# Forward and backward of a spectral mixer with a channel MLP: eight early w2^T blocks with ScalarE copies, input-gradient passes ordered tile by tile, and three small moves

## The chip, the cores and the metric

One core of one Trainium2 chip. The metric is the device time of one execution in microseconds. The kernel before took 1412.49 us (median of 3 runs, 1410.25 to 1417.26). The engines are called as in the profile: PE is TensorE (matmul) and PEld its weight loads, DVE is VectorE, ACT is ScalarE, POOL is GpSimd, SP is SyncE; SP and POOL issue most of the DMAs.

## The reference

The kernel computes one forward pass and all gradients of it (2048 tokens, width 1024, hidden width 3584, bfloat16).

```python
mod = (silu(c) @ w_mod).reshape(1, 6, 1, -1)          # sa, ca, ga, sb, cb, gb
h = layernorm(x) * (1 + ca) + sa
x = x + ga * irfft2(rfft2(h) * (w_r + 1j * w_i))      # spectral part
h = layernorm(x) * (1 + cb) + sb
x = x + gb * (gelu(layernorm(h) @ w1 + b1) @ w2 + b2) # channel MLP
out, vjp = jax.vjp(f, A_x, A_w_r, A_w_i, B_w1, B_b1, B_w2, B_b2, c, w_mod)
return out, *vjp(grad_out)
```

## The kernel before, in words

Everything is written with Tile, a framework in which the program states operations on tiles and a planner lays out, before the run and by its own estimates of durations, the order of the instructions of each engine, the engine of each `nc.any` operation (ScalarE or VectorE), and the waits. Each engine then works strictly through its list. The program steers the planner by its own order (earlier lines have priority), by `tc.high_priority()`, by `tc.issue_after(ins)` and by `behind(ins, later)` (both put an instruction after another on one engine). Tiles with the same `tag` share one place in memory: a new tile waits for the last reader of the one before it. PSUM has the tags `s` and `d` with two banks each and `f` with four.

The stages, in the order of time:

1. *Start (0 to 122 us).* Six products `silu(c) @ w_mod` (`mod_block`), grad_out transposed and scaled into `gBoT`, and the first blocks of `ph_part` (L809). One block `fc` of `ph_part` is grad_out x w2^T for 128 hidden columns: four token groups j, each of 8 matmuls 128x512 at L814 into an `f` bank (`pp`), a copy to SBUF (L820, tiles `pho` and `phr`, `phr` being the place of every fourth block), and one POOL store to `d_ph`. The weights come through a ring of four `wt` places, by a transposing DMA of SP (`load_w2t`). `PH_EARLY = 6` (L824) blocks stand in a loop that also loads the weights four blocks ahead, a seventh stands alone behind it (L834), and its last matmul is `early_pe`. Meanwhile VectorE and ScalarE normalise x in four chunks (`ln_dve`, `ln_mix`, `norm_act`) and VectorE folds them by symmetry into `fbuf` (`fold_tok`, `fold_d`, `fold_pair`, all through L194). Chunk 2 is complete only after the last `fold_pair`.
2. *Spectral part, forward (to 222 us).* `spectral_core`: the `pu` matmuls (L531, L538) read `fbuf`; the first group is put behind `early_pe`. Blocks of `ph_part` that are written further down (L897 on) are used by the planner as filling wherever a spectral matmul is not ready.
3. *Rest of `ph_part` (to 344 us)*, then the MLP forward (to 733 us): `z_block` (pz, L951, PSUM `s` and `d` in turn; gelu and its derivative on ScalarE and VectorE) and `bo_pass` (pbo, L1005), in a hand-written order. At the end of each `bo_pass`, `pa` (an `s`/`d`/`f` bank; `d` here) holds column sums that go into `gacc` (its memory is called w2sD in the profile): L1027 copies it for b = 0.
4. *Input-gradient passes (733 to 941 us).* `pg_pass(b, h)`, L1099: for token block b (4) and half h (2), four PSUM tiles `pgs[i]` are summed over 7 groups g of hidden columns, 4 matmuls each (L1105). A step is one (g, i), four matmuls; a pass has 28 steps, g outer and i inner. The operand `gzs[b, g]` is loaded by SP into a ring of eight places (L1081). At the end ScalarE copies the four tiles with a row sum (L1121, `gn3a`, `gn3b`). For b < 2 and h = 1 ScalarE also sums each `gzs[b, g]` for the bias gradient (L1115). For b > 0 column sums (`acc3a`, L217) are put between steps at fixed places. Successive passes take their PSUM tiles from six banks in turn, so the third tile of a pass needs the bank of an early tile of the pass before. VectorE and ScalarE meanwhile work on `ln_bwd` (L1199 to L1204).
5. *Weight gradient of w2 and spectral part, backward (to 1200 us and beyond)*, with 16-matmul pieces (`fill(n)`) of the w2 and w1 weight gradients (L1239, L1464) put between. `consume_bwd(i, ...)`, i = 0 to 3: unfolds, multiplies with the normalised x (`tmp`, called ct), LayerNorm backward, store; then `fill((4, 7, 6, 8)[i])`, the column sum `halves_sum(accCA, tmp)` (L217, 8 matmuls), `fill(2)`.
6. *End (to 1411 us).* `accSA` sums (L214), `sr` (L1519, tag `px0`, which the fourth chunk's x, called xt, holds before it) takes them scaled by ScalarE (L1521); then the remaining w1 pieces, whose results are copied at L1468 and stored.

Of the kernel before, what the change touches and what calls it, by code (L numbers as in the profile page):

```python
# [10 lines left out]
FP32 = mybir.dt.float32  # L11
# [6 lines left out]
P = 128  # L18
S = 2048
D = 1024  # L20
# [3 lines left out]
NFC = F // P  # L24
KH = D // 2
# [5 lines left out]
NB = 4  # L31
# [4 lines left out]
def kernel(  # L36
# [24 lines left out]
    nc = tc.nc  # L61
# [4 lines left out]
    reg = ctx.enter_context(tc.tile_pool(name="reg", bufs=1))  # L66
# [12 lines left out]
    def ps_f(name):  # L79
        return psum.tile([P, 512], FP32, tag="f", name=name, bufs=4)  # L80
# [44 lines left out]
    def chunk_rows(dt, i):  # L125
        return dt[4 * i * P:4 * (i + 1) * P, :].rearrange("(q p) d -> p q d", p=P)
# [213 lines left out]
    def load_w2t(fc):  # L340
        w2t_in[0] = nc.sync.dma_start_transpose(out=wt[:, fc % 4], in_=B_w2[fc * P:(fc + 1) * P, :])
        w2ts.append(w2t_in[0])
# [461 lines left out]
    last_pe = [None]  # L804

    def ordered():
        return tc.issue_after(last_pe[0].ins)

    def ph_part(fc, js):  # L809
        ph2 = phs[fc % 4]  # L810
        for j in js:
            pp = ps_f("pp")
            for cch in range(NDC):
                last_pe[0] = nc.tensor.matmul(pp[:], lhsT=wt[:, fc % 4, cch, :], rhs=gBoT[j][:, cch, :],  # L814
                                              start=(cch == 0), stop=(cch == NDC - 1))
            q = (0, 2, 3, 1)[j]
            ov = ph2[:, :, q * P:(q + 1) * P]
            pv = pp[:, :].rearrange("p (i w) -> p i w", w=P)
            with tc.high_priority():
                nc.any.tensor_copy(out=ov, in_=pv)  # L820
        if js[-1] == 3:
            nc.gpsimd.dma_start(out=d_ph[fc * P:(fc + 1) * P, :], in_=ph2.rearrange("p i w -> p (i w)"))

    PH_EARLY = 6  # L824
    late_mods = [(r, h) for r in (2, 3, 4) for h in range(2)]
    for fc in range(PH_EARLY):
        ph_part(fc, (0, 1, 2, 3))
# [3 lines left out]
                for r, h in late_mods[3 * (fc // 2 - 1):3 * (fc // 2)]:  # L831
                    mod_block(r, h)

    ph_part(PH_EARLY, (0, 1, 2, 3))  # L834
    early_pe = last_pe[0]

    for i in range(4):
# [56 lines left out]
            w1s.append(wtile)  # L894

    PH_KEEP = NFC - 4
    for fc in range(PH_EARLY + 1, NFC):  # L897
        if fc >= PH_EARLY + 4:
            load_w2t(fc)
            load_w1({24: 1, 25: 1, 27: 5}.get(fc, 0))  # L900
        ph_part(fc, (0, 1, 2, 3) if fc < PH_KEEP else (0, 1))
# [10 lines left out]
    gacc = px1t[:, 1].rearrange("p a b -> p (a b)").bitcast(FP32)  # L912
# [76 lines left out]
    def bo_pass(b, h):  # L989
        cs_ = slice(h * KH, (h + 1) * KH)  # L990
        pbs = [((ps_s, ps_d)[k % 2] if (b, h) == (NB - 1, 0) else ps_f)("pbo") for k in range(4)]
        for i in range(4):
            with ordered():
                last_pe[0] = nc.tensor.matmul(pbs[i][:], lhsT=ones_bf[32 * i:32 * i + 1, :],
                                              rhs=b2_row[32 * i:32 * i + 1, cs_], start=True, stop=False,
                                              tile_position=(32 * i, 0))
        for g in range(7):
            n = (2 * b + h) * 7 + g
            w2_load(n + 3 if b == NB - 1 else n)
            wp = w2p[n % 4]  # L1000
            hh = hh_slots[(b * 7 + g) % 11]
            for i in range(4):
                for k in range(4):
                    with ordered():
                        last_pe[0] = nc.tensor.matmul(pbs[i][:], lhsT=hh[:, k, i * P:(i + 1) * P], rhs=wp[:, k, :],  # L1005
                                                      start=False, stop=(g == 6 and k == 3))
            if g < 6:
                yield
        bo, x1t, go = (otile[0][:, k] for k in range(3))
        nc.sync.dma_start(out=x1t, in_=chunk_rows(d_x1, b)[:, :, cs_])  # L1010
        load_tok_half(go, grad_out, b, h)
        for i in range(4):
            with tc.high_priority():
                last_ev[0] = nc.scalar.copy(out=bo[:, i, :], in_=pbs[i][:])
        tt(go, go, bo, ALU.mult)
        tt(bo, bo, bcn(gb_row[:, cs_], 4), ALU.mult)
        tt(bo, bo, x1t, ALU.add)
        store_tok_half(out_0, bo, b, h)

        yield  # L1020
        pa = (ps_f if (b, h) in ((NB - 2, 1), (NB - 1, 1)) else ps_d)("pa")
        for i in range(4):
            with ordered():
                last_pe[0] = nc.tensor.matmul(pa[32 * i:32 * (i + 1), :], lhsT=ones_bf[:, 0:32], rhs=go[:, i, :], start=True, stop=True)
        with tc.high_priority():
            if b == 0:
                nc.vector.tensor_copy(out=gacc[:, cs_], in_=pa[:])  # L1027
            else:
                tt(gacc[:, cs_], gacc[:, cs_], pa[:], ALU.add)

# [65 lines left out]
    last_pg = [None]  # L1096
    sums_in = [[], [], []]

    def pg_pass(b, h, pool, before=lambda: ExitStack()):  # L1099
        pgs = [pool(k)("pg") for k in range(4)]  # L1100
        for g in range(7):
            for i in range(4):
                for k in range(4):
                    with before():
                        last_pg[0] = nc.tensor.matmul(pgs[i][:], lhsT=gzs[b, g][:, k, i * P:(i + 1) * P],  # L1105
                                                      rhs=w1Ts[g][:, k, h * KH:(h + 1) * KH],
                                                      start=(g == 0 and k == 0), stop=(g == 6 and k == 3))
                    last_pe[0] = last_pg[0]
                g0 = 3 if b == NB - 1 else 2
                if b > 0 and h == 0 and (g, i) in ((g0, 0), (g0 + 1, 2), (g0 + 2, 2)):  # L1110
                    for ins in sums_in[g - g0]:
                        behind(ins, last_pg[0])
                    sums_in[g - g0].clear()
            for k in range(4 if b < 2 and h == 1 else 0):
                nc.scalar.activation(out=gzs[b, g][:, k, :], in_=gzs[b, g][:, k, :], func=ACT.Identity,  # L1115
                                     accum_out=gb1_acc[:, g * 4 + k, b:b + 1])
            if g < 6:
                yield
        for i in range(4):
            with tc.high_priority():  # L1120
                nc.scalar.activation(out=gn3_of(b)[:, i, h * KH:(h + 1) * KH], in_=pgs[i][:], func=ACT.Identity,  # L1121
                                     accum_out=g_sums[b][:, h, i:i + 1])
        yield
# [248 lines left out]
    def consume_bwd(i, o4, tmp, tmp2, n1, eb):  # L1372
        if i == 0:
            accCA.append(ps_s("accCA"))
            nc.vector.tensor_copy(out=sacc, in_=eb[:, 0, :])
        elif i == 2:
            tt(sacc, sacc, eb[:, 0, :], ALU.add)
        unfold_d(o4, tmp)
        unfold_tok(o4, tmp)
        load_tok(n1, A_x, i, nc.gpsimd)  # L1380
        with tc.issue_after(last_po[0].ins):
            norm_act(n1, n1, 0, i)
        tt(tmp, o4, n1, ALU.mult)
# [92 lines left out]
    def fill(n):  # L1476
        for _ in range(n):
            next(todo)
        done[0] += n
# [36 lines left out]

    accSA = [ps_d("accSA0"), ps_d("accSA1")]
    colsum(accSA, sacc, True, True)
    sr = reg.tile([P, 2, 1, D], FP32, name="sr", tag="px0")  # L1519
    for h in range(2):  # L1520
        nc.scalar.mul(out=sr[0:1, 0, 0, h * KH:(h + 1) * KH], in_=accSA[h][0:1, :], mul=8.0)  # L1521
    unfold_d(sr[0:1, 0], sr[0:1, 1])
# [48 lines left out]
```

## Time and profile before

| what | value |
|---|---|
| median of 3 runs | 1412.49 us (1410.25 to 1417.26) |
| profiled execution | 1412.42 us, span 1410.6 us |
| mean granted TensorE clock | 0.992 |
| DMA | 333.22 MB, mean 236 GB/s |
| TensorE busy in slices of 35 us | 5, then 9 or more of ten throughout, 8 in one that holds the start of the spectral part |

The span runs from the first to the last instruction; the rest of the execution's time lies around it. In an order of time a row has start, length in us, engine, line, operation, out<-in, shape and count; in brackets stands the idle time before the first of them, and what ended it. A row of a list of waits has who waited, for whom, total us, times, longest. A row of windows has the stretch, its length, and the busy time of each engine in it, then the granted clock, the share of the DMA engines and GB/s.

### The profile page before, as it was taken

What the parts mean: (1) busy time and instruction counts of PE and PEld (TensorE: products, weight loads), DVE (VectorE), ACT (ScalarE), POOL (GpSimd) and SP (SyncE); (2) the same over time, 40 slices, a digit from 0 to 9 for tenths busy, and PEclk for the clock granted to TensorE, in tenths of its full rate; (3) what the DMA queues carried; (4) which work ended last, traced back from release to release, by engine and by line L of the source; (5) the groups of instructions that cost most, each with busy time, mean ns of one, the idle gap of its engine ahead of it and who ended that gap; (6) DMA issues with size and microseconds to landing.
All of it is one profiled execution on the core that took longest, in us unless ns stands there. A gap on an engine that the chain in (4) does not pass through costs nothing. (4 is left out here: it accounts for less than half of the span.)

```text
span 1410.6 us, 18696 instructions
## 1 busy us (share of the span) xinstructions
PE 1374.2 (97%) x6963; PEld 664.5 (47%) x6963; DVE 1072.4 (76%) x1507; ACT 739.2 (52%) x1059; POOL 351.2 (25%) x436
## 2 busy tenths in 40 slices
PE   5998999999999999999999999999999999999999
PEld 2545565444444444444444444444544565444444
DVE  5897889987978777887620688999498757979960
ACT  4774667667877765665314583243622444434311
POOL 5510623201112122112210010112345330322341
PEclk8899999999999999999999999999999999999999
DMA  9972666899787777696999499996689996897971
GB/s 330 301 234 57 176 165 200 265 283 350 256 258 242 229 242 249 189 287 224 298 271 232 138 237 321 259 259 209 197 265 288 261 253 173 218 250 189 286 270 38
DMA packets 361265, 333.22 MB, mean 236 GB/s; under 512 B 208026, under 2 KB 303152, under 8 KB 361046
## 3 DMA queue, kind: packets, MB, share of 16 engines
q1 hardware_dynamic: 319990, 206.01, 55.9%
q0 software_dynamic: 35424, 120.78, 24.5%
q10 hardware_dynamic: 5760, 5.25, 1.2%
q8 instruction: 54, 0.88, 0.3%
q14 instruction: 37, 0.30, 0.1%
HBM read 166.77 MB, written 115.92 MB: 200 GB/s over the span
## 5 line engine op out<-in xcount | busy, mean ns | idle before, releaser
L1105 PE MATMUL pg<-w1T,gzr 128*128 128x512 bf16 x896 | 196.0, 379 | 2.8 <-ACT gn3b L1121 2.8
L814 PE MATMUL pp<-gBoT,wt 128*128 128x512 bf16 x896 | 197.9, 380 | 0.8 <-DVE phr L820 0.4
L1464 PE MATMUL gw1acc<-gzh,n3n 128*128 128x512 bf16 x640 | 140.0, 379 | 0.2 <-DVE gwo L1468 0.2
L1105 PEld LDWEIGHTS <-gzr 128*128 128x128 bf16 x896 | 86.6, 98 | 111.1 <-issue 8.5
L1464 PEld LDWEIGHTS <-n3n 128*128 128x128 bf16 x896 | 87.3, 98 | 107.1 <-issue 3.3
L951 PEld LDWEIGHTS <-w 128*128 128x128 bf16 x896 | 87.2, 98 | 107.0 <-issue 2.5
L814 PEld LDWEIGHTS <-wt 128*128 128x128 bf16 x896 | 87.5, 98 | 104.0 <-issue 1.5
L951 PE MATMUL pz<-n3Tb,w 128*128 128x512 bf16 x448 | 99.2, 379 | 1.0 <-DVE w2sD L1027 1.0
L951 PE MATMUL pz<-n3Ta,w 128*128 128x512 bf16 x448 | 98.7, 379 | 0.0
L1005 PEld LDWEIGHTS <-hhA 128*128 128x128 bf16 x608 | 59.0, 98 | 73.1 <-issue 2.8
L1239 PE MATMUL gw2acc<-gB,hhsA 128*128 128x512 bf16 x416 | 92.2, 379 | 0.0
L954 ACT ACTIVATE gt<-pz,b_col 128x512 bf16<-128x512 f32 x112 | 72.8, 683 | 33.2 <-PE pz L951 33.0
L962 ACT ACTIVATE gt<-gt 128x2048 bf16<-128x2048 bf16 x28 | 53.5, 1911 | 64.8 <-DVE gt L194 64.8
L194 DVE TENSOR_TENSOR gt<-gt,gt 128x2048 bf16<-128x2048 bf16 x56 | 68.6, 1224 | 19.8 <-ACT gt L964 18.5
L194 DVE TENSOR_TENSOR ct<-ct 128x2048 bf16<-128x2048 bf16 x68 | 80.6, 1218 | 0.9
L1468 ACT CAST gwo<-gw1acc 128x512 bf16<-128x512 f32 x50 | 28.4, 581 | 89.3 <-PE gw1acc L1464 78.5
L1247 ACT CAST gwo<-gw2acc 128x512 bf16<-128x512 f32 x40 | 23.3, 584 | 93.6 <-PE gw2acc L1239 90.5
L1239 PEld LDWEIGHTS <-hhsA 128*128 128x128 bf16 x416 | 40.7, 98 | 47.4
L1470 POOL DMA_DIRECT2D out_dram<-gwo x53 | 29.2, 554 | 129.8 <-DVE gwo L1468 67.6
L1464 PE MATMUL gw1acc<-gzu,n3n 128*128 128x512 bf16 x256 | 55.6, 379 | 1.2 <-ACT gwo L1468 1.2
L958 ACT ACTIVATE gt<-gt 128x2048 bf16<-128x2048 bf16 x28 | 53.5, 1909 | 2.1 <-DVE hhC L194 1.3
L964 ACT ACTIVATE gt<-gt 128x2048 bf16<-128x2048 bf16 x28 | 53.4, 1907 | 0.4
(347 smaller groups left out, 2558.4 us busy)
## 6 DMA issues: line engine op xcount, KB each, us to landing
gzr<-d_gz SPq DMA_DIRECT2D x28, 512.0 KB
wblk<-in_w_mod_dram SPq DMA_DIRECT2D x12, 1024.0 KB
out_dram<-otl POOLq DMA_DIRECT2D x48, 256.0 KB, 4.9
d_ph<-pho POOLq DMA_DIRECT2D x21, 512.0 KB, 6.0
d_hh<-hhA POOLq DMA_DIRECT2D x19, 512.0 KB, 5.1
w<-in_B_w_dram SPq DMA_DIRECT2D x7, 1024.0 KB
hhC<-d_ph SPq DMA_DIRECT2D x14, 512.0 KB
w2sA<-d_ph SPq DMA_DIRECT2D x14, 512.0 KB
```

The costliest lines, as they stand in the source:

```text
L194: return nc.vector.tensor_tensor(out=out, in0=a, in1=b, op=op)
L814: last_pe[0] = nc.tensor.matmul(pp[:], lhsT=wt[:, fc % 4, cch, :], rhs=gBoT[j][:, cch, :], start=(cch == 0), stop=(cch == NDC - 1))
L951: last_pe[0] = nc.tensor.matmul(pz[:], lhsT=w1s[g][:, cch, k * P:(k + 1) * P], rhs=n3T[:, cch, :], start=(cch == 0), stop=(cch == NDC - 1))
L954: z_in = nc.scalar.activation(out=zb[:, k, :], in_=pz[:], func=ACT.Identity, bias=b1_col[:, fc:fc + 1], scale=1.0)
L958: nc.scalar.activation(out=av, in_=zb, func=ACT.Square)
L962: nc.scalar.activation(out=sg, in_=bv, func=ACT.Sigmoid, scale=2.0 * GK)
L964: nc.scalar.activation(out=bv, in_=bv, func=ACT.Sigmoid, scale=-2.0 * GK)
L1005: last_pe[0] = nc.tensor.matmul(pbs[i][:], lhsT=hh[:, k, i * P:(i + 1) * P], rhs=wp[:, k, :], start=False, stop=(g == 6 and k == 3))
L1105: last_pg[0] = nc.tensor.matmul(pgs[i][:], lhsT=gzs[b, g][:, k, i * P:(i + 1) * P], rhs=w1Ts[g][:, k, h * KH:(h + 1) * KH], start=(g == 0 ...
L1239: nc.tensor.matmul(acc[:], lhsT=hh_of(fc)[:, t, :], rhs=gBs[t // 4][:, t % 4, h * KH:(h + 1) * KH], start=(t == 0), stop=(t == NT - 1))
L1464: nc.tensor.matmul(acc[:], lhsT=n3ns[t // 4][:, t % 4, cch * P:(cch + 1) * P], rhs=gz2[t // 8][:, t % 8, :], start=(t == 0), stop=(t == NT ...
L1470: eng.dma_start(out=out_4[cch * P:(cch + 1) * P, fg * 512:(fg + 1) * 512], in_=ob)
```

## The change

- `PH_EARLY` is 8: eight blocks stand in the early loop (which loads the weights of blocks 4 to 11), the one alone behind it is gone, and `early_pe` is the last matmul of the eighth. Copies of blocks 3 to 7 are made by ScalarE; those of the others stay with `nc.any`. The two groups of `mod_block` stay behind blocks 3 and 5.
- `gacc` of b = 0 is copied by ScalarE instead of VectorE.
- `pg_pass` for b > 0 takes the groups in blocks (0, 1), (2), (3), (4, 5, 6); within a block the tile i is outer and the group inner. So the first two groups are summed tile by tile, and the last three: tile 0 is complete after step 19 of 28 instead of 25, tile 1 after 22, tile 2 after 25, tile 3 at the end. The column sums keep their step numbers. The bias sums of b = 1 follow each block; those of groups 4 to 6 come together. b = 0 keeps the old order.
- In `consume_bwd` the third chunk's column sum comes one piece later.
- `sr` takes the place `smb` (held before by `eb`, the halves that the first and third chunk produce) instead of `px0`.

```diff
-                nc.any.tensor_copy(out=ov, in_=pv)
+                (nc.scalar.copy if 3 <= fc < PH_EARLY else nc.any.tensor_copy)(out=ov, in_=pv)
...
-    PH_EARLY = 6
+    PH_EARLY = 8
...
-    ph_part(PH_EARLY, (0, 1, 2, 3))
     early_pe = last_pe[0]
...
-    for fc in range(PH_EARLY + 1, NFC):
+    for fc in range(PH_EARLY, NFC):
...
-                nc.vector.tensor_copy(out=gacc[:, cs_], in_=pa[:])
+                nc.scalar.copy(out=gacc[:, cs_], in_=pa[:])
...
-        for g in range(7):
-            for i in range(4):
-                for k in range(4):
-                    with before():
-                        last_pg[0] = nc.tensor.matmul(pgs[i][:], ...)
-                    last_pe[0] = last_pg[0]
-                g0 = 3 if b == NB - 1 else 2
-                if b > 0 and h == 0 and (g, i) in ((g0, 0), (g0 + 1, 2), (g0 + 2, 2)):
-                    for ins in sums_in[g - g0]:
-                        behind(ins, last_pg[0])
-                    sums_in[g - g0].clear()
-            for k in range(4 if b < 2 and h == 1 else 0):
+        blocks = ((0, 1), (2,), (3,), (4, 5, 6)) if b > 0 else tuple((g,) for g in range(7))
+        steps = [(g, i, i == 3 and g == block[-1] and block) for block in blocks for i in range(4) for g in block]
+        for n, (g, i, ends) in enumerate(steps):
+            for k in range(4):
+                with before():
+                    last_pg[0] = nc.tensor.matmul(pgs[i][:], ...)
+                last_pe[0] = last_pg[0]
+            n0 = 12 if b == NB - 1 else 8
+            if b > 0 and h == 0 and n - n0 in (0, 6, 10):
+                at = (n - n0 + 2) // 5
+                for ins in sums_in[at]:
+                    behind(ins, last_pg[0])
+                sums_in[at].clear()
+            if not ends:
+                continue
+            for g, k in [(g, k) for g in ends for k in range(4 if b < 2 and h == 1 else 0)]:
                 nc.scalar.activation(out=gzs[b, g][:, k, :], ..., accum_out=gb1_acc[:, g * 4 + k, b:b + 1])
-            if g < 6:
+            if ends[-1] < 6:
                 yield
...
-        fill((4, 7, 6, 8)[i])
+        fill((4, 7, 7, 8)[i])
         halves_sum(accCA[0], tmp, i == 0, i == 3)
-        fill(2)
+        fill(1 if i == 2 else 2)
...
-    sr = reg.tile([P, 2, 1, D], FP32, name="sr", tag="px0")
+    sr = reg.tile([P, 2, 1, D], FP32, name="sr", tag="smb")
```

More of the change, by code (lines that the diff above doesn't have):

```diff
@@ L1100, in pg_pass @@
         pgs = [pool(k)("pg") for k in range(4)]
-        for g in range(7):
-            for i in range(4):
-                for k in range(4):
-                    with before():
-                        last_pg[0] = nc.tensor.matmul(pgs[i][:], lhsT=gzs[b, g][:, k, i * P:(i + 1) * P],
-                                                      rhs=w1Ts[g][:, k, h * KH:(h + 1) * KH],
-                                                      start=(g == 0 and k == 0), stop=(g == 6 and k == 3))
-                    last_pe[0] = last_pg[0]
-                g0 = 3 if b == NB - 1 else 2
-                if b > 0 and h == 0 and (g, i) in ((g0, 0), (g0 + 1, 2), (g0 + 2, 2)):
-                    for ins in sums_in[g - g0]:
-                        behind(ins, last_pg[0])
-                    sums_in[g - g0].clear()
-            for k in range(4 if b < 2 and h == 1 else 0):
+        blocks = ((0, 1), (2,), (3,), (4, 5, 6)) if b > 0 else tuple((g,) for g in range(7))
[3 more added lines that the diff above has]
+                with before():
+                    last_pg[0] = nc.tensor.matmul(pgs[i][:], lhsT=gzs[b, g][:, k, i * P:(i + 1) * P],
+                                                  rhs=w1Ts[g][:, k, h * KH:(h + 1) * KH],
+                                                  start=(g == 0 and k == 0), stop=(g == 6 and k == 3))
+                last_pe[0] = last_pg[0]
[8 more added lines that the diff above has]
+            for g, k in [(g, k) for g in ends for k in range(4 if b < 2 and h == 1 else 0)]:
                 nc.scalar.activation(out=gzs[b, g][:, k, :], in_=gzs[b, g][:, k, :], func=ACT.Identity,
                                      accum_out=gb1_acc[:, g * 4 + k, b:b + 1])
-            if g < 6:
+            if ends[-1] < 6:
                 yield
```

## The prediction

> **What bounds the kernel now.** I read the busy table of the page first, then the list of waits for TensorE, then the order of time around each wait.
>
> ```profile
> span 1410.6 us, 18696 instructions
> PE 1374.2 (97%) x6963; PEld 664.5 (47%) x6963; DVE 1072.4 (76%) x1507; ACT 739.2 (52%) x1059; POOL 351.2 (25%) x436
> ```
> ```profile
> PE pu L538 <- DVE fbuf L194: 5.1, 1, 5.1
> PE pg L1105 <- ACT gn3b L1121: 2.8, 1, 2.8
> ...
> PE accCA L217 <- DVE ct L194: 1.6, 1, 1.6
> ...
> PE gw1acc L1464 <- ACT gwo L1468: 1.2, 1, 1.2
> ...
> PE pz L951 <- DVE w2sD L1027: 1.0, 1, 1.0
> ```
>
> TensorE is busy for 97% and does the same work in both kernels (no matmul is added or taken away), so only its 1410.6 - 1374.2 = 36.4 us of idle time can change, and time lost in a cold clock. The second fence has line waited for, total, times, longest. These five waits are 5.1 + 2.8 + 1.6 + 1.2 + 1.0 = 11.7 us, and each sits at a line that the diff touches or feeds. The first costs more than its idle time:
>
> ```profile
> 116.70:121.90 5.20, 0.09 (x2) 0.04 (x2) 5.04 (x7) 0.00 (x0) 0.00 (x0) 0.92 0.29 109
> 121.90:127.90 6.00, 6.00 (x27) 3.96 (x28) 1.77 (x1) 2.92 (x5) 0.00 (x0) 0.50 0.01 1
> ...
> 918.30:921.80 3.50, 3.50 (x17) 1.61 (x17) 2.13 (x6) 2.92 (x7) 0.00 (x0) 1.00 0.50 195
> ```
>
> The columns: the stretch, its length, busy time (and instructions) of PE, PEld, DVE, ACT and POOL, granted clock, DMA. The clock is 0.92 over the wait (half speed for 0.16 x 5.2 = 0.8 us, so it fell about 4.3 us after TensorE had stopped), then 0.50 for 6.0 us, which does 3.0 us of work: 3.0 lost. After the 2.8 us wait (last row) it is 1.00. So the wait at pu costs 5.1 + 3.0 = 8.1 us, and all five 14.7.
>
> **The change part by part.**
>
> *Eight blocks ahead of the spectral part.*
>
> ```profile
> 99.97 7.07 PE L814 MATMUL pp<-gBoT,wt 128*128 128x512 bf16 x32
> 106.88 0.38 PE L538 MATMUL pu<-smA,fbuf 128*128 128x256 bf16 x2
> 107.10 9.66 PE L814 MATMUL pp<-gBoT,wt 128*128 128x512 bf16 x44
> 121.87 1.46 PE L538 MATMUL pu<-smA,fbuf 128*128 128x256 bf16 x6 [5.11 <-DVE fbuf L194]
> ```
> ```profile
> 77.00:122.00 45.00, 39.89 (x187) 18.02 (x185) 44.44 (x51) 25.79 (x41) 2.67 (x5) 0.99 0.58 183
> ```
> ```profile
> 77.17 2.29 DVE L194 TENSOR_TENSOR fbuf<-fbuf,rows 128x4096 bf16<-128x4096 bf16 x1 [0.98 <-ACT fbuf L514]
> ```
> ```profile
> L820 DVE CAST pho<-pp x4: 667/682/690, 70.5 to 91.9; 128x512 bf16<-128x512 f32 x4
> L820 DVE CAST phr<-pp x3: 677/684/685, 73.8 to 79.4; 128x512 bf16<-128x512 f32 x3
> ```
> ```profile
> L820 ACT CAST pho<-pp x12: 562/584/597, 68.6 to 116.0; 128x512 bf16<-128x512 f32 x12
> ```
> ```profile
> 107.07 8.36 SPq L341 DMA_TRANSPOSE wt<-in_B_w_dram  x2
> 134.65 6.12 SPq L686 DMA_TRANSPOSE smi<-d_SF  x4
> ```
>
> The seventh early block ends at 107.0. The program's order then has two pu matmuls and 44 pp matmuls: all 32 of block 7 and 12 of block 8, taken forward as filling. So block 7 runs ahead of the wait already, and pinning it gains nothing by itself: TensorE reaches 107.0 + 7.07 = 114.1 with all eight done, and how many of the 12 are still taken forward (0 to 2.6 us at 216 ns) depends on where the planner now expects the folds. The moved block brings 32 matmuls, four copies, one POOL store and the transposes of blocks 10 and 11 on SP's queue; those two are issued at 107.07 already, and SP has nothing else until 134.65, so nobody is behind them.
>
> What can gain is VectorE. Of the copies of blocks 3 to 7 it makes five (three phr copies from 73.8 to 79.4, and the two last pho copies, up to 91.9; the two pho copies before them are block 2's). From 77 to the end of the folds at 121.8 (0.1 before pu's second start) it is busy for 44.4 of 45.0 us, so the three copies in that stretch count, some 0.6 each (682 ns less the overlap with the next): 1.8 us. The other two lie ahead of the 0.98 us in which it waits for ScalarE, and free nothing. On ScalarE the five cost 0.58 each, 2.9 in all. If they hide in its pauses the folds end 1.8 earlier; if all five stand ahead of the normalisations, 2.9 later. I take 1.8 earlier, since ScalarE is busy for 25.8 of those 45 us, and waits 3.4 us for VectorE ahead of the last normalisation:
>
> ```profile
> 94.99 0.58 ACT L820 CAST pho<-pp 128x512 bf16<-128x512 f32 x1 [0.59 <-PE pp L814]
> 98.94 3.51 ACT L514 ACTIVATE fbuf<-x,stats 128x1024 bf16<-128x1024 bf16 x3 [3.36 <-DVE stats L194]
> ```
>
> With half of the 12 fill matmuls (1.3 us) the wait runs from 115.4 to 120.1: 4.7 us in place of 5.1, and the gain in place is 1.8 less the 1.3 us of work not taken forward, 0.5. Whether the clock falls is worth six times that. It fell 4.3 us into a 5.1 us wait and not in one of 2.8; 4.7 is a little beyond 4.3, 3.4 (all 12 kept) below it. It is near even; I take that it stays up, 3.0. Term: -3.5. Ends: -8.1 (wait gone), and +5.6 (folds 2.9 later, 2.7 us less work in front).
>
> The Trainium skill ("TensorE: Matmul & The Clock Gate", "Part 1: The HAM clock gate") says that the clock halves after one idle window of about 3.4 us that runs freely. The half clock in the row above agrees. By that rule a 4.7 us wait would hold a whole window in (4.7 - 3.4) / 3.4, about 4 cases of 10, an estimate from the page; the term would then be -2.3 on average. The skill's page "ScalarE: Activation LUTs" ("Rules for kernel authors") speaks against the move, since it gives simple element work to VectorE; here the same copy takes 584 ns on ScalarE and 682 on VectorE, and the measurement decides.
>
> *Input-gradient passes tile by tile.*
>
> ```profile
> 909.24 6.22 PE L1105 MATMUL pg<-w1T,gzr 128*128 128x512 bf16 x28
> 918.30 2.97 PE L1105 MATMUL pg<-w1T,gzr 128*128 128x512 bf16 x13 [2.84 <-ACT gn3b L1121]
> ```
> ```profile
> 916.43 1.24 ACT L1203 ACTIVATE got<-n2u,sc 128x1024 bf16<-128x1024 bf16 x1 [3.76 <-DVE sc L1202]
> 917.58 0.58 ACT L1121 ACTIVATE gn3b<-pg 128x512 bf16<-128x512 f32 x1
> ```
>
> The last row group of pass (3,0) has 20 matmuls of that pass (ending 909.24 + 20 x 0.216 = 913.6) and 8 of the next; then the next pass wants tile 0's bank, whose copy stands behind a ScalarE instruction that waits for VectorE. In the new order tile 0 is complete nine steps (9 x 0.87 = 7.8 us) before the pass ends, at 905.8, and the next pass wants the bank two steps (1.7 us) later. Even with the copy left at 917.58 the wait would shrink by 1.7; I expect the copy to be queued ahead. What it costs: the last three groups of gz must all be there when the closing part starts.
>
> ```profile
> 898.89 5.35 PE L1105 MATMUL pg<-w1T,gzr 128*128 128x512 bf16 x24
> ```
> ```profile
> 896.56 1.08 SPq L1081 DMA_DIRECT2D gzr<-d_gz  x2
> ```
> ```profile
> d_hh<-hhA POOLq DMA_DIRECT2D x19, 512.0 KB, 5.1
> ```
>
> 898.89 is step 13, so step 17 (group 5) falls at 902.4 and step 18 (group 6) at 903.2, where they were wanted at steps 20 and 24. Their loads are issued at 896.56 and half a us later; the nearest row for 512 KB lands after 5.1 us: 901.7 and 902.2. Spare: under 1 us. I allow 0.8 for lateness over three blocks. ScalarE's bias sums of block 1 also come in one run of twelve at the end, behind the copies; the loads that wait for them are needed half a pass later. Term: -2.0; ends -2.8 and +3 (three late loads of 1 us).
>
> *fill.* The third accCA sum moves one piece of 16 matmuls (3.5 us) later; TensorE's queue behind it keeps one piece.
>
> ```profile
> 1264.73 2.29 DVE L194 TENSOR_TENSOR ct<-ct,xt 128x4096 bf16<-128x4096 bf16 x1
> 1267.07 0.61 PE L217 MATMUL accCA<-ct,ones_bf 128*32 128x512 bf16 x8 [1.59 <-DVE ct L194]
> ```
>
> It would start at 1265.5 + 3.5 = 1269.0, after 1267.0. Term: -1.6, ends -1.6 and 0.
>
> *sr in smb.*
>
> ```profile
> 1255.75 1.23 DVE L194 TENSOR_TENSOR ct<-eb 128x2048 bf16<-128x2048 bf16 x1 [3.65 <-DMA out_dram<-ct,xu]
> ```
> ```profile
> 1311.86 0.59 PE L214 MATMUL accSA<-otl,ones_bf 128*128 128x512 bf16 x2
> ```
> ```profile
> 1325.89 1.06 ACT L1521 ACTIVATE sr<-accSA 1x512 f32<-1x512 f32 x2 [8.90 <-DVE ct L194]
> 1326.86 1.99 ACT L1468 CAST gwo<-gw1acc 128x512 bf16<-128x512 f32 x4
> ```
>
> sr waits for the last reader of px0 and four result copies queue behind it; TensorE waits 1.2 for the first. smb's last reader is the fourth chunk's subtraction of the eb halves, at 1255.75, and accSA is there at 1312.5. Term: -1.2, ends -1.2 and 0.
>
> *gacc by ScalarE.*
>
> ```profile
> 438.46 0.40 PE L1024 MATMUL pa<-otile,ones_bf 128*32 128x512 bf16 x4
> ```
> ```profile
> 444.46 0.68 DVE L1027 COPY w2sD<-pa 128x512 f32<-128x512 f32 x1
> ```
> ```profile
> 441.37 1.91 ACT L962 ACTIVATE gt<-gt 128x2048 bf16<-128x2048 bf16 x1 [3.71 <-DVE gt L194]
> 443.31 1.91 ACT L964 ACTIVATE gt<-gt 128x2048 bf16<-128x2048 bf16 x1
> ```
>
> pa is there at 438.9. If ScalarE takes it in the 3.71 us pause, the 1.0 goes. If it stands behind the sigmoid at 443.31 (to which the old copy's place on VectorE corresponds) the bank comes free at 445.2 + 0.6, against 445.1 before: +0.7. Between them I take 0; ends -1.0 and +0.7.
>
> Sum: -3.5 - 2.0 - 1.6 - 1.2 + 0 = -8.3. The profiled execution took 1412.42 us (span 1410.6 and 1.8 around it), 0.1 below the median 1412.49. 1412.4 - 8.3 = **1404.1**.
>
> **Rivals.**
>
> *The wait at pu only moves* (clock falls again, gain there 0.5 or nothing): -4.8 to -5.3, **1407.4**. For it: the planner's error in the folds' end stays what it is, and 4.7 is beyond 4.3. Against: ScalarE has pauses and VectorE none.
>
> *It goes wholly* (fill matmuls kept and folds 3 us earlier): -12 to -13, **1400**.
>
> *ScalarE's copies stand ahead of the normalisations: slower.* All 20 copies of blocks 3 to 7 are on the engine that VectorE waits for. If four (2.3 us) precede each of three chunks' normalisations, the folds end 7.0 - 1.8 = 5.2 later, at 127.1, with 2.7 less work in front: +7.9 against -4.8 elsewhere, **1415.5**. It decides from folds that end later than 121.8 + 4.8 - 2.7 = 123.9. For it: the 0.98 us wait at 77.17. Against: ScalarE is idle for four tenths of that stretch.
>
> *It does not do what it says:* the order of every later stage is planned anew, and as much is lost to new waits: **1412**.
>
> **How the numbers follow.** Forecast 0.40 (1401 to 1406), moved wait 0.30, wholly gone 0.08, eaten 0.12, slower rival 0.10 (1413 to 1421). 0.5% is 7.1 us, about what a measurement tells from no change: faster means below 1405.4. The forecast gives 0.36 of that, the moved wait 0.05, the wholly gone 0.08: 0.49. Slower than 1419.5 is half of the slower rival and 0.02 of the rest: 0.07. Same: 0.44. The range 1399 to 1415 leaves out about 0.15.
>
> **What would show it.** Granted clock 1.00 right after the first pu wait, and that wait under 4.3 us; no L820 copy on VectorE between 70 and 115; pg, accCA and gw1acc gone from the list of waits, no pg wait on DMA. It is wrong if ScalarE's copies delay the folds past 123.9, or if new waits of microseconds stand in stages that the diff does not touch.

## The result, and the profile after

The changed kernel is slower: **1420.4 us** (median of 10 runs, 1417.1 to 1422.7) against 1413.1 us for the kernel before (10 runs beside them, 1410.3 to 1417.3). The ratio is **1.005, 95% interval 1.0036 to 1.0064**: about 7.3 us lost where 8.3 were forecast to be won. The time lies above the forecast's whole range of 1399 to 1415, and on the other side of no change. The profiled execution of the changed kernel took 1422.2 us.

The first lines of its page: TensorE does the same 6963 matmuls, is busy 3.4 us longer (1377.6 against 1374.2, time in a slower clock), and idle for 1420.4 - 1377.6 = 42.8 us, 6.4 more.

```profile
span 1420.4 us, 18695 instructions
...
PE 1377.6 (97%) x6963; PEld 663.6 (47%) x6963; DVE 1068.4 (75%) x1500; ACT 743.2 (52%) x1066; POOL 356.0 (25%) x436
```

Its list of waits for TensorE (line waited for, total, times, longest):

```profile
PE pm L278 <- DMA wblk<-in_w_mod_dram: 12.3, 6, 4.0
PE pg L1105 <- DMA gzr<-d_gz: 8.6, 2, 6.8
PE pu L538 <- DVE fbuf L194: 3.4, 1, 3.4
PE pz L950 <- ACT w2sD L1026: 2.2, 1, 2.2
...
PE gw2acc L1242 <- DVE gB L194: 1.7, 1, 1.7
```

Of the five waits that the prediction listed, those for gn3b, ct (accCA) and gwo (gw1acc) are gone; pu's is shorter, 3.4 in place of 5.1; pz's has grown from 1.0 to 2.2 and is now for ScalarE. Two are new: 8.6 us for the loads of gzr, and 1.7 us for VectorE's gB. The order of time on TensorE puts the large one in the closing part of pass (2,0), at steps 17 and 18 of its 28 (counted from 0; groups 5 and 6):

```profile
861.19 1.89 PE L1105 MATMUL pg<-w1T,gzr 128*128 128x512 bf16 x4 [6.77 <-DMA gzr<-d_gz]
...
864.92 1.87 PE L1105 MATMUL pg<-w1T,gzr 128*128 128x512 bf16 x4 [1.84 <-DMA gzr<-d_gz]
```

Four matmuls there take 1.9 us, twice the usual: the clock is at half. The stretches of the changed kernel with half clock (length, busy time and instructions of PE, PEld, DVE, ACT, POOL, granted clock, DMA):

```profile
858.70:869.10 10.40, 6.07 (x18) 1.57 (x19) 2.99 (x10) 0.69 (x2) 0.00 (x0) 0.51 1.12 274
445.30:449.30 4.00, 3.98 (x11) 1.50 (x11) 3.90 (x4) 2.44 (x5) 1.41 (x1) 0.57 0.80 242
121.30:125.00 3.70, 3.70 (x18) 2.31 (x19) 1.77 (x1) 1.76 (x3) 0.00 (x0) 0.54 0.01 2
```

Busy time at half clock does half the work: 3.0 us lost in the first stretch, some 1.7 in each of the others. An account of the two profiled executions from these rows and those of the prediction: pg +8.6 + 3.0 - 2.8 (gn3b); gw2acc +1.7; pz +1.2 + 1.7; pu -1.7 and 1.3 less half clock; accCA and gw1acc -1.6 - 1.2; pm, which the diff doesn't touch, +2.5. Together +10.1, where the two executions differ by 1422.2 - 1412.4 = 9.8. The account takes the larger waits alone; the others nearly cancel.

Why gzr came late is seen on SP's queue. In the kernel before, three loads are issued one behind the other, and then a transpose of hb:

```profile
842.71 1.92 SPq L1081 DMA_DIRECT2D gzr<-d_gz  x3
849.11 3.55 SPq L1275 DMA_TRANSPOSE hb<-d_hh  x1
```

Counted from the first of the 28 loads, these three are groups 4, 5 and 6 of block 2. In the changed kernel two loads (groups 3 and 4) are followed by the transpose and the load of au, and only then by the loads of groups 5 and 6:

```profile
842.56 1.06 SPq L1080 DMA_DIRECT2D gzr<-d_gz  x2
850.72 2.44 SPq L1278 DMA_TRANSPOSE hb<-d_hh  x1
...
853.88 1.00 SPq L1080 DMA_DIRECT2D gzr<-d_gz  x2
```

Between 843.6 and 850.7 SP issues nothing: the transpose writes a home of hb that an earlier turn is still storing into d_hhT. SP's own list of waits from 836 to 870:

```profile
SPq L1278 <- DMA d_hhT<-hb: 7.2, 2, 6.7
```

So the two loads stood 6.7 us behind an instruction that waited for something else. They were issued at 853.9 and 854.4; the new order of the passes asks for them from about 854. Their places were free before that: ScalarE's bias sums of groups 4 and 5 of block 1, which held these places, end by about 840.6, 3 us before SP falls idle. So what held the loads back in this execution is the order in which the planner had put SP's queue, not the places themselves.

**The theory** that the experiments were to test: the run of twelve bias sums at the end of pass (1,1) frees the homes of groups 5 and 6 later, so the planner places the transpose first, and the closing part of pass (2,0) asks for both groups earlier (steps 17 and 18 in place of 20 and 24). **Rival 1:** the early part (eight pinned blocks, ScalarE's copies) shifts the plan of all later stages, and the wait comes from that. **Rival 2:** the earlier need alone is enough, whatever SP's queue holds.

### The profile page after: what moved, and what is told of

Same layout as the page of the kernel before. It is cut to its first block, busy times and chain, and to the rows that moved or that the text cites. A ratio compares the mean times of both kernels' runs of the same rounds, so it can differ in the third digit from the quotient of the medians.

```text
span 1420.4 us, 18695 instructions
## 1 busy us (share of the span) xinstructions
PE 1377.6 (97%) x6963; PEld 663.6 (47%) x6963; DVE 1068.4 (75%) x1500; ACT 743.2 (52%) x1066; POOL 356.0 (25%) x436
```

## The experiments

"Before + x" is the kernel before with one part of the change; "after - x" the changed kernel without it. Ratios are to the kernel before, run beside each on the same chip. Two executions of one kernel differ by several us, so single times carry little and the rows of the profile more.

### Which part: after - passes, before + passes

The first run leaves pg_pass as it was, and keeps all the rest of the change; the second changes pg_pass alone:

```diff
-        for g in range(7):
-            for i in range(4):
...
+        blocks = ((0, 1), (2,), (3,), (4, 5, 6)) if b > 0 else tuple((g,) for g in range(7))
+        steps = [(g, i, i == 3 and g == block[-1] and block) for block in blocks for i in range(4) for g in block]
...
```

> The changed kernel with the input-gradient passes in the old order, all its other parts kept. Theory (the new order of the passes moves the loads of groups 5 and 6 of block 2 behind a transpose on SP's queue): the 8.6 us wait of pg for gzr and its 10.4 us of half clock go, the 2.8 us wait of pg for gn3b comes back; 1420.4 - 11.6 + 2.8 = about 1411. Rival 1 (the eight pinned blocks and the copies shift the plan of the later stages, and the pg wait comes from that): the wait stays, and the time with it, 1418 to 1423. Rival 2 (the earlier need of the two groups, not the queue) expects the same here as the theory.

> The kernel before with the input-gradient passes in the new order alone. Theory: the pg wait for gzr at the end of pass (2,0), 8 to 9 us with half clock behind it, less the 2.8 us wait for gn3b: 1413 + 11.6 - 2.8 + up to 2 of lag met later = 1421 to 1424. Rival 1 (the pinned blocks move the later stages): no pg wait for gzr above 1 us, 1410 to 1411.

After - passes: 1411.4 us, ratio 0.9992 (0.9979 to 1.0005). Before + passes: 1420.8 us, ratio **1.0059** (1.0036 to 1.0081). The waits of the second:

```profile
PE pg L1106 <- DMA gzr<-d_gz: 9.5, 3, 7.3
...
PE gw2acc L1243 <- DVE gB L194: 1.7, 1, 1.7
```

The new order of the passes alone makes the whole loss, with the same two new waits. Rival 1 falls: without the passes the pg wait for gzr is gone, with the pinned blocks in place. The first run also says what the other parts are worth together: -1.1 us by its ratio (between -3.0 and +0.7), where the prediction's terms for them add up to -6.3.

### Queue order or earlier need

Two kernels cross the two causes. One has the new order of the passes, with block 2's loads put ahead of the transpose; the other the old order of the passes, with the load of group 5 put behind the transpose (turn_in holds the last transpose; the lines that set it are left out):

```diff
...
+            if b == 2:
+                behind(turn_in[0], gz_in[0])
```
```diff
...
             for g in range(7):
-                load_gz(b, g)
+                with tc.issue_after(turn_in[0].ins) if (b, g) == (2, 5) else ExitStack():
+                    load_gz(b, g)
```

> The kernel before with the input-gradient passes in the new order, and one order added on SP's queue: the transpose of hb that stood ahead of the loads of groups 5 and 6 of block 2 is issued behind block 2's loads. Theory (the queue): the pg wait for gzr falls from 8.6 to under 1.5 us and the clock stays up, 1410 to 1414. Rival 2 (TensorE wants the two groups some 5 us earlier than they can be loaded, whatever stands ahead of them on SP): wait 5 us or more, 1418 or more. The bias sums of block 1 end 3 us later than in the kernel before, so a wait of 1 to 3 us would be theirs.

> The kernel before, its passes in the old order, with the loads of groups 5 and 6 of block 2 put behind the transpose of hb on SP's queue, as the changed kernel has them. Theory (queue order and earlier need together): the groups are wanted at steps 20 and 24 of the pass, 3 to 6 x 0.87 = 2.6 to 5.2 us later than in the new order, so a wait of 3 to 6 us for gzr in pass (2,0) and perhaps half clock behind it: 1416 to 1422. Rival 2 (the earlier need is all): no wait, 1411 to 1415.

The second kernel does less than its expectation says. The edit names group 5 alone, and one load stands behind the transpose and the load of au (issued at 849.06), not two; TensorE's wait at step 20 ends with it, and group 6's load went out ahead of them:

```profile
849.64 0.50 SPq L1081 DMA_DIRECT2D gzr<-d_gz  x1
```

From the lists of waits, of the first and then of the second:

```profile
PE pg L1106 <- DMA gzr<-d_gz: 2.9, 1, 2.9
```
```profile
PE pg L1105 <- DMA gzr<-d_gz: 4.1, 1, 4.1
```

| wait of pg for gzr, time (ratio) | old order: groups wanted at steps 20, 24 | new order: at steps 17, 18 |
|---|---|---|
| loads of groups 5 and 6 ahead of the transpose | none, 1412.2 (kernel before) | 2.9 us, 1414.2 (1.0013; 0.9998 to 1.0028) |
| behind it | 4.1 us, 1413.2 (1.0003; 0.9987 to 1.0019); group 5 alone behind it | 9.5 us, 1420.8 (1.0059; 1.0036 to 1.0081) |

Each cause alone gives a wait of 3 or 4 us, both together 9.5 us (1.5 of them for group 3, whose load goes out later too), and only both together cost time that can be measured. What the old order would lose with both loads behind the transpose wasn't run, so the lower left field may be too small. The repaired queue takes back 6.5 of the 8.6 us between the kernel before and before + passes. The first run's expectation of under 1.5 us was too low: rival 2 holds for the 2.9 us that are left (here four loads go out in a row, since group 3's is still 10 us later than in the kernel before). In the second, the 4.1 us wait doesn't show in the time, and its list has no wait for gn3b any more. The rows of pass (3,0) tell why. First TensorE's stretch of 16 pg matmuls (steps 19 to 22) in the kernel before, then the same stretch in this kernel, and ScalarE's first copy of a bank there:

```profile
904.71 3.63 PE L1105 MATMUL pg<-w1T,gzr 128*128 128x512 bf16 x16
```
```profile
908.96 3.63 PE L1105 MATMUL pg<-w1T,gzr 128*128 128x512 bf16 x16
```
```profile
916.61 0.57 ACT L1121 ACTIVATE gn3b<-pg 128x512 bf16<-128x512 f32 x1
```

TensorE is 4.3 us later, but ScalarE's copy isn't (917.58 in the kernel before, by the prediction's row): the instruction ahead of it waits for VectorE, which didn't wait for TensorE. So the 2.8 us that TensorE waits there in the kernel before are time that it has in hand in block 2, and lateness costs only beyond it. By this reading waits of 3 or 4 us are nearly free. In before + passes the stretch behind the wait has 3.5 us of work at half clock, 1.7 lost:

```profile
857.20:864.10 6.90, 3.50 (x8) 0.86 (x8) 1.36 (x4) 0.00 (x0) 0.00 (x0) 0.51 1.09 302
```

With the new wait for gB this makes 9.5 + 1.7 + 1.7 - 2.8 = 10.1; accCA's 1.6 us are also missing from this execution's list, which leaves 8.5, where 8.6 were measured.

The same repair in the changed kernel itself:

> The changed kernel with block 2's loads of gzr put ahead of the transpose of hb on SP's queue, nothing else. Theory (the queue order is the larger half of the loss): the pg wait for gzr falls from 8.6 to about 3 us, as it did beside the kernel before, and the time by 5 to 8 us: 1412 to 1416. Rival (in the changed kernel the bias sums end 3 us later and hold the loads back by themselves): the wait stays above 6 us, 1418 or more.

1414.2 us, ratio 1.0009 (0.9992 to 1.0026): 6.2 less than the changed kernel, as the theory had it. The wait fell by less: three waits for gzr, 5.0 us in all, between the theory's 3 and the rival's 6. The longest is now for group 6, one step behind the place of the 6.77 us:

```profile
858.77 1.86 PE L1105 MATMUL pg<-w1T,gzr 128*128 128x512 bf16 x4 [3.05 <-DMA gzr<-d_gz]
```

### What is left with the queue repaired

The next kernel has the new passes except pass (1,1), so that the bias sums stand in their old places, and with them SP's order:

```diff
-        blocks = ((0, 1), (2,), (3,), (4, 5, 6)) if b > 0 else ...
+        blocks = ((0, 1), (2,), (3,), (4, 5, 6)) if b > 0 and (b, h) != (1, 1) else ...
```

> The kernel before with the passes in the new order, except pass (1,1), which keeps the old one, so that its bias sums come in their old places and SP's queue keeps the old order. Theory (the late bias sums and the queue order make the loss): the pg wait for gzr is under 1.5 us, the 2.8 us wait for gn3b is gone, 1.7 us of it come back as gw2acc's wait for VectorE: 1410 to 1413. Rival (TensorE's earlier need of groups 5 and 6 in pass (2,0) is enough by itself): a wait of 3 us or more in pass (2,0), 1414 to 1419.

SP's order is that of the kernel before (three loads in a row, then the transpose), with no order written by hand. So it was the new order of pass (1,1) that moved the loads. Whether its run of twelve bias sums did it, or its matmuls, which read groups 4 to 6 to the end of the pass, no run here parts. First SP's rows, then TensorE's in pass (2,0):

```profile
845.65 1.91 SPq L1081 DMA_DIRECT2D gzr<-d_gz  x3
853.13 2.93 SPq L1279 DMA_TRANSPOSE hb<-d_hh  x1
```
```profile
850.54 1.04 PE L1106 MATMUL pg<-w1T,gzr 128*128 128x512 bf16 x4 [0.33 <-DMA gzr<-d_gz]
853.53 1.04 PE L1106 MATMUL pg<-w1T,gzr 128*128 128x512 bf16 x4 [1.95 <-DMA gzr<-d_gz]
856.71 1.89 PE L1106 MATMUL pg<-w1T,gzr 128*128 128x512 bf16 x4 [2.14 <-DMA gzr<-d_gz]
```

Three waits, 4.4 us in all: the rival's size, and the theory's under 1.5 was wrong; the time, 1411.6 us, ratio 1.0007 (0.9994 to 1.0021), is not above the kernel before. The rows show the mechanism: the loads of groups 4, 5 and 6 are issued within 1.5 us, and the three steps that wait for them begin 3.0 and 3.2 us apart. That is the pace at which 512 KB land there, beside transposes and stores that fill the DMA engines (share 0.99 from 845 to 857 us): 512 KB in 3.1 us are 170 GB/s. The old order takes a new group every four steps, 3.5 us; the closing part takes three groups in two steps, 1.7 us.

The last kernel of this group takes the closing part away and keeps the new opening and the repaired queue:

```diff
-        blocks = ((0, 1), (2,), (3,), (4, 5, 6)) if b > 0 else ...
+        blocks = ((0, 1), (2,), (3,), (4,), (5,), (6,)) if b > 0 else ...
```

> The kernel before with the new beginning of the passes (two groups tile by tile) and the old ending (group by group), and block 2's loads put ahead of the transpose on SP's queue. Theory (with the queue repaired, what is left of the wait comes from the closing part: it asks for groups 4, 5 and 6 within two steps, 1.7 us, though their loads land some 3 us apart): no pg wait for gzr above 1 us, the wait of pg for gn3b at 2.8 to 3.2 us again: 1410 to 1414. Rival (the loads land late whoever asks): a wait of 2 us or more for gzr in pass (2,0).

```profile
PE pg L1106 <- ACT gn3b L1125: 1.7, 1, 1.7
...
PE pg L1106 <- DMA gzr<-d_gz: 0.3, 1, 0.3
```

0.3 us for gzr, and the wait for gn3b is back, at 1.7 us in place of 2.8: as the theory had it but for that size. 1410.8 us, ratio 0.9993 (0.9978 to 1.0008): the smallest median of the twelve, and not to be told from the kernel before.

### What the passes could have won

The filling piece and sr alone, and then with the new order of the passes in the last block of rows only (b == NB - 1), where there are no bias sums and SP's order stays:

```diff
-        fill((4, 7, 6, 8)[i])
+        fill((4, 7, 7, 8)[i])
...
-        fill(2)
+        fill(1 if i == 2 else 2)
...
-    sr = reg.tile([P, 2, 1, D], FP32, name="sr", tag="px0")
+    sr = reg.tile([P, 2, 1, D], FP32, name="sr", tag="smb")
```

> The kernel before with the moved piece of filling and sr in its new home alone. Theory (as the prediction): the wait of accCA (1.6 us in the kernel before) and that of gw1acc (1.2) go and nothing comes in their place: 2.8 less, 1409 to 1411, a ratio of 0.998. Rival (something later takes them up, or they are within what runs differ by): ratio 1.000.

> As the run before it, and the new order of the passes in the last block of rows alone, where no bias sums are made and SP's queue keeps its order. Theory: no pg wait for gzr above 1 us; the 2.8 us wait of pg for gn3b goes, and the half clock that followed waits of 2.9 to 3.2 us there in three runs with it; VectorE's lag comes back as a wait of 1 to 2 us of gw2acc for gB. Together 1.1 to 2.8 less than the run before it: 1407 to 1410, ratio 0.997. Rival (the new order loses as much in the last block too): a gzr wait in pass (3,0), and no gain over the run before it.

Without the passes: 1411.6 us, ratio 0.9993 (0.9979 to 1.0006), where 2.8 us less were expected. accCA's wait is gone. gw1acc's wait for ScalarE is gone too, but TensorE waits 1.1 us some 50 us earlier, for a result copy on VectorE (0.2 near that place in the kernel before).

With the passes: 1413.6 us, ratio 1.0008 (0.9995 to 1.0022), no gain over the other run. The lists of waits of the two, the one without the passes first:

```profile
PE pg L1105 <- ACT gn3b L1121: 3.0, 1, 3.0
...
PE gw1acc L1464 <- DVE gwo L1468: 1.1, 1, 1.1
```
```profile
PE gw2acc L1243 <- DVE gB L194: 3.9, 1, 3.9
```

The 3.0 us at the change of tile come back 27 us later as 3.9 us for VectorE, with half clock behind them (0.51 from 945.2 us on) that the other run doesn't have. The expectation of 1 to 2 us there was too low. VectorE, not the copy of the bank, is what TensorE is ahead of in this stage; it came to that place 3 us sooner, and waited there.

### The early part and gacc

The pinned blocks with ScalarE's copies alone; the same with block 3's copies left to the planner (4 <= fc in place of 3 <= fc); and gacc's copy alone:

```diff
-                nc.any.tensor_copy(out=ov, in_=pv)
+                (nc.scalar.copy if 3 <= fc < PH_EARLY else nc.any.tensor_copy)(out=ov, in_=pv)
...
-    PH_EARLY = 6
+    PH_EARLY = 8
...
```
```diff
-                nc.vector.tensor_copy(out=gacc[:, cs_], in_=pa[:])
+                nc.scalar.copy(out=gacc[:, cs_], in_=pa[:])
```

> The kernel before with the eight pinned blocks and ScalarE's copies alone. From the start of ScalarE's table load ahead of the first fold to the start of the last fold on VectorE the traces have 51.9 us in the kernel before and in three kernels with its early part, 52.3 in the changed one. Theory (ScalarE's copies of block 3 stand between the four normalisations of one chunk, and VectorE waits as long as the copies that it was spared): 52.3 again, so the wait of pu isn't shortened by the edit. Rival (the prediction: VectorE is spared 1.8 us): 50.1. Time 1411 to 1414 by the theory, 1409 by the rival.

> As the run with the eight pinned blocks and the copies, but block 3's copies left where the planner puts them (ScalarE takes those of blocks 4 to 7): no copy stands between the four normalisations of the first chunk. Theory: VectorE's wait ahead of its first fold is 1.0 us again, the two copies of block 4 (0.6 us each in a full queue) are gone from VectorE, and the distance from the table load to the last fold falls from 51.9 to 50.6. Rival (copies between the normalisations of the second chunk cost as much as those of the first): 51.9 or more. Time 1409 to 1413 in both: 1 us is within what two runs differ by.

> The kernel before with gacc's first copy on ScalarE alone. Theory (the copy stands behind a 1.9 us sigmoid on ScalarE's queue): the wait of pz grows from 1.0 to between 1.7 and 2.2 us, and costs up to 1.7 us more if the clock halves after it; 1413 to 1416. Rival (what is seen in the changed kernel comes from the other parts): the wait of pz stays at 1.0 us or goes.

The folds are measured from ScalarE's table load to VectorE's last fold, which leaves out when the stage began (that differs by up to 1.6 us among the profiled kernels). First ScalarE's and VectorE's rows of the kernel before:

```profile
69.23 1.28 ACT L479 ACT_TABLE_LOAD   x1
...
72.52 4.62 ACT L514 ACTIVATE fbuf<-x,stats 128x1024 bf16<-128x1024 bf16 x4
```
```profile
121.12 0.69 DVE L194 TENSOR_TENSOR fbuf<-fbuf,sb_saf 128x1024 bf16<-128x1024 bf16 x1
```

Then those of the changed kernel:

```profile
68.19 1.28 ACT L479 ACT_TABLE_LOAD   x1
...
71.48 2.36 ACT L514 ACTIVATE fbuf<-x,stats 128x1024 bf16<-128x1024 bf16 x2
73.74 0.56 ACT L820 CAST phr<-pp 128x512 bf16<-128x512 f32 x1
74.20 1.24 ACT L514 ACTIVATE fbuf<-x,stats 128x1024 bf16<-128x1024 bf16 x1
75.35 0.57 ACT L820 CAST phr<-pp 128x512 bf16<-128x512 f32 x1
75.81 1.25 ACT L514 ACTIVATE fbuf<-x,stats 128x1024 bf16<-128x1024 bf16 x1
```
```profile
77.09 2.29 DVE L194 TENSOR_TENSOR fbuf<-fbuf,rows 128x4096 bf16<-128x4096 bf16 x1 [3.13 <-ACT fbuf L514]
...
120.47 0.69 DVE L194 TENSOR_TENSOR fbuf<-fbuf,sb_saf 128x1024 bf16<-128x1024 bf16 x1
```

51.9 us before (121.12 - 69.23), 52.3 after. Two of the copies stand between the four normalisations that VectorE's first fold waits for, and its wait grew from 0.98 to 3.13. The first fold starts 1.0 us later (8.9 us behind the table load; 77.17 - 69.23 = 7.9 before), and from there the folds take 0.6 us less, 43.4 in place of 44.0. With the early part alone it is 52.3 again (67.98 to 120.26), as the theory had it; its one time, 1412.7 us, is like that of the kernel before. With block 3's copies left alone the wait is 0.98 again and the folds take 51.0 (69.42 to 120.40): 0.9 better, where the theory had 1.3. That kernel took 1415.4 us in its one run, with a wait of 3.1 us that is in none of the others, 195 us later on, for ScalarE's copy of a much later block (L820). One run each doesn't tell what these kernels' times are worth.

For gacc ScalarE's rows show the order that the prediction gave as its worse end, here in the changed kernel:

```profile
442.89 1.91 ACT L963 ACTIVATE gt<-gt 128x2048 bf16<-128x2048 bf16 x1
444.71 0.57 ACT L1026 COPY w2sD<-pa 128x512 f32<-128x512 f32 x1
```

Alone it makes pz's wait 1.6 us in place of 1.0, with no half clock behind it, a little under the 1.7 to 2.2 that the theory had; 1411.5 us in one run.

## Why the prediction was wrong, point by point

- **TensorE's idle time is what can change, and the clock after it.** Right: the account of both adds up to 10.1 us, where the two executions differ by 9.8.
- **Passes: -2.0, ends -2.8 and +3.** This is the step that failed, at +8.6 (before + passes against its kernel before). What failed is the allowance for late loads: 0.8 us over three blocks, 3 at the worst, where one block alone cost 8.6 to 9.5 us of waiting. In block 3, for which the prediction worked out the landing, it held (no wait in the changed kernel, 0.5 us in the kernel with the new order in the last block alone). For block 2 it had a single sentence: "ScalarE's bias sums of block 1 also come in one run of twelve at the end, behind the copies; the loads that wait for them are needed half a pass later." Half a pass is about right (step 17 of 28). The conclusion that it is enough was wrong: with pass (1,1) in the new order the planner put the loads of groups 5 and 6 behind a transpose that waits 6.7 us, and what else stands on SP's queue in block 2 does not enter the prediction. The landing time was also too short: 5.1 us was taken from a store of POOL, while the three loads of the kernel with pass (1,1) left alone, issued at 845.7, 846.6 and 847.1, released their steps 4.9, 6.9 and 9.6 us later. The spare time of "under 1 us" was a sign that there was no room for a queue.
- **The gain itself, -2.8.** Also wrong, as a term: the wait for gn3b goes as forecast, and comes back as 1.7 to 3.9 us for gB, as VectorE is what is late next, and TensorE is only about 3 us ahead of it there. The prediction didn't look for what comes next after that wait.
- **pu: -3.5.** Mis-sized: VectorE was spared its copies, and the rival's mechanism, ScalarE's copies ahead of normalisations, took that back (+0.4 us at the end of the folds in place of -1.8). The 12 matmuls of filling stayed at 12. The 3.0 us for a clock that stays up came out nowhere: all 14 traces, with pu waits of 3.0 to 5.1 us, have half clock right behind that wait. What the profiled run won at pu comes from the start of its stage (TensorE reached the wait at 117.9 us in place of 116.8, and ScalarE's table load began 1.0 us earlier) and from a shorter half clock, and both differ as much between kernels with the early part of the kernel before (pu's wait is 3.0 to 5.1 us in those).
- **accCA and gw1acc: -2.8.** Right that both waits go, wrong that nothing replaces them: -1.0 by the ratio, between -3.0 and +0.8 by its interval.
- **gacc: 0, ends -1.0 and +0.7.** The worse end came true: +0.6 alone. In the changed kernel it was +1.2, and half clock behind it.
- **The rivals.** "As much is lost to new waits" (1412) had the kind of cause right and its size too small; the loss was not spread over all later stages but stood in one place that the diff touches. The mechanism of the slower rival was at work, but the folds end 0.4 us later where it had 5.2. That 1420.4 lies in that rival's range (1413 to 1421) is therefore luck: the time came from another stage. The rival of a wait that goes wholly was also summed wrongly: folds 3 us earlier leave 2.1 of the 5.1 us, which makes -10.8 and not -12 to -13.

## What to carry to other kernels

A load's latest moment isn't its landing time alone: read the whole issuing queue at that place, and for each instruction ahead of the load what it waits for, since a change that frees a buffer 3 us later can put the load behind a wait of 7. An order that finishes one tile early must have all its operands together at the end; where they are loaded at the pace at which they were used, pulling the last three forward turns the pace of the loads into a wait. And a wait that is taken away on an engine which meets another late engine 30 us later has been moved: ask what the two engines' distance is at the next place where they meet.

## What the runs showed of the hardware that was not expected

The clock after a wait is not a matter of the wait's length alone. The wait for gn3b at the same place, in six kernels: 2.84, 2.8 and 3.05 us were followed by full clock, 2.92, 3.12 and 3.16 by half clock. In the kernel with the early part alone even a wait of 2.06 us, for accCA, was followed by half clock. So a wait of 2 to 3 us costs itself, and in some executions 1.7 us more. The prediction's reading, that the clock falls 4.3 us after TensorE stops and waits under that are safe, was drawn from one execution and does not hold.

What decides shows when the waits are laid on the clock's own steps. In all 14 traces every stretch of one clock (but the last, which the end cuts) lasts a multiple of 3.41 us, so the clock changes only at steps of that length, and where the steps lie differs from execution to execution. Take every step at full clock and TensorE's busy share in it: all 50 steps with a share up to 0.40 are followed by half clock, 11 of the 16 between 0.40 and 0.48, and none of the 5559 above that. (The ends of matmuls are modelled in these traces, so the shares are rough.) Three waits show it, each with its row and the step that holds most of it. In the kernel with the filling piece and sr alone, the 3.05 us are split between two steps; this one is busy for 1.70 of 3.42 us, and the clock stays up:

```profile
918.16 22.61 PE L1105 MATMUL pg<-w1T,gzr 128*128 128x512 bf16 x102 [3.05 <-ACT gn3b L1121]
```
```profile
916.44:919.86 3.42, 1.70 (x8) 0.77 (x8) 3.38 (x7) 3.40 (x9) 0.53 (x1) 1.00 1.04 377
```

In the kernel with gacc alone, 2.92 us lie in one step, which is busy for 0.49 us, and the next step is at half clock:

```profile
917.81 4.44 PE L1105 MATMUL pg<-w1T,gzr 128*128 128x512 bf16 x12 [2.92 <-ACT gn3b L1121]
```
```profile
914.57:917.98 3.41, 0.49 (x3) 0.14 (x2) 3.38 (x7) 2.04 (x4) 0.14 (x1) 1.00 1.07 374
917.98:921.40 3.42, 3.42 (x9) 1.22 (x8) 2.05 (x6) 2.75 (x7) 0.39 (x1) 0.50 0.69 265
```

In the kernel with the early part alone, the 2.06 us lie wholly in one step, busy for 1.35 of 3.41 us, and that is enough:

```profile
1267.47 1.04 PE L217 MATMUL accCA<-ct,ones_bf 128*32 128x512 bf16 x8 [2.06 <-DVE ct L194]
```
```profile
1264.10:1267.51 3.41, 1.35 (x11) 0.53 (x12) 3.29 (x3) 0.00 (x0) 0.00 (x0) 1.00 1.09 241
1267.51:1270.92 3.41, 3.19 (x13) 0.97 (x14) 3.41 (x7) 0.00 (x0) 0.00 (x0) 0.50 1.02 230
```

From these shares an estimate for a single wait: about 2 us of idle time within one step (0.6 x 3.41) bring the clock down, so a wait of over some 4 us always does, wherever it falls, and one of 2 to 4 us does by chance. The 4.7 us that the prediction had at pu would have been among the first. The Trainium skill ("TensorE: Matmul & The Clock Gate", "Part 1: The HAM clock gate") has a window of about 3.4 us that runs freely, which agrees with one length of wait giving both clocks; it asks for a whole idle window, and with that waits of 2.06, 2.2 and 2.92 us followed by half clock do not agree.
